# Windowed attention and a routed MLP: stores on GpSimd's queue, an early identity, full-width transposes, and two more engines in program order

## The chip, the cores and the metric

The kernel runs on one core of a Trainium2 chip. TensorE multiplies matrices, VectorE and ScalarE do element-wise work, GpSimd does slower general work and issues some DMAs, and SyncE only issues DMAs. Each engine works through its own list of instructions in order and waits on semaphores for the others. The metric is the time of one launch in microseconds (us), as the median of several runs. The profile is one such execution, and its times count from the start of its span.

## The reference

Four batches of eight heads, 768 positions, 64 numbers a head. Each query sees itself, the 127 positions before it, and four "sink" positions at the start. A routed MLP then works on 128 rows of each batch.

```python
scores = scale * np.matmul(q, k.transpose(0, 1, 3, 2))
keep = is_sink | in_window
a = softmax(np.where(keep, scores, -1e9))
x = np.matmul(a, v)                          # heads side by side: [B, S, 512]
scores = np.einsum('bsd,d->bs', x, w_gate)
for b in range(B):
    top_idx = np.argpartition(-scores[b], capacity)[:capacity]
    xe = x[b, top_idx]
    ye = np.maximum(xe @ w1, 0.0) @ w2
    out[b, top_idx] = x[b, top_idx] + sigmoid(scores[b, top_idx])[:, None] * ye
```

The rows that aren't chosen go out as x.

## The kernel before, in words

**Units.** The attention is cut in 24 units (b, j): batch b, block j of 128 queries. In unit u the loop gives out, in this order: at j = 0 the loads of the next batch (`load_qk`, `load_v`, and for batch 0 three weight loads); the scores of the *next* unit, whose exponentials ScalarE writes into `pt` (L274); the sink part of the output (`pv_sinks`, L291); the casts of the next batch's q and k for the head pairs that `prep` names; the output product `pv` for two groups of four heads (L301), each followed by VectorE's reciprocal `rz` (L307) and product `x` (L310); the sink scores at j = 0; the transposes of the next batch; two casts of MLP weights in units (1,0) to (1,3) (`cast_w`, L212 and L215); `compare` for the unit before; one step of the MLP of the batch before (`moe_steps`); and `finish_block`.

**Casts and transposes.** q and k come in as 32-bit numbers (`kf`, `qf`) and are cast to bf16 (`kb`, `qb`), two heads to a tile: by ScalarE and VectorE for batch 0 (L107, L108), by GpSimd with a select that selects everything for the others (L111). TensorE then turns each 128x64 piece (L227), one head into the upper and one into the lower 64 partitions of a PSUM tile; VectorE copies the turned k out (`KT`, L232, and a small piece `ksk`, L236), ScalarE the turned q (`QT`, L234).

**Sinks.** `load_v` loads v in six pieces (L120). After the second it also loads the sink rows `vsr` (L126, two small loads), and VectorE multiplies them with a selection mask into `vsk` (L127), which `pv_sinks` reads from j = 2 on:

```python
            if c == 1:
                raw = vsr[b % 2]
...
                nc.vector.tensor_tensor(
                    out=st.vsk[:, :, 0:D], in0=raw[:, :].unsqueeze(1).to_broadcast((128, 4, D)),
```

**Finish and choice.** `finish_block` stores x (L315), for the last batch also makes a bf16 copy on GpSimd (L319), and reduces x with the gate weights to a score per row (`junk`, `scol`, L322). `compare` spreads the scores over the partitions (`bc` by TensorE, `sbc` by ScalarE, L330) and counts on VectorE which rows rank higher (`cm`, L333). The steps of `moe_steps` run in units j = 1 to 5 of the next batch: the ranks and a selection matrix `E` (L345 to L358); the row numbers `idx` and the gather of the chosen rows from the output in memory (`xe`, L374, by GpSimd); their transposes `xeT` (L380); the two products (L390, L396); and a gated add to memory (L400). `moe_last` does it for the last batch.

**Buffers.** x has four buffers, the accumulators `xg` three, other PSUM tiles five, raw q and k three each, `kb` and `qb` three each, v and `vsr` two.

**What sets the order.** In the loop, TensorE's instructions keep the order in which the program gives them. All other engines, and SyncE's DMA queue, are ordered by a planner: it models the run, and at each step gives an engine the earliest instruction of the program that it then holds to be ready. The instructions ahead of the loop are all ordered by it. All loads and stores are issued by SyncE; the gathers and scatters by GpSimd.

```python
    with tc.manual_schedule(engines={ENG.PE}):
        start_state(st0)
        keep_warm(14)
```

`keep_warm` (L76) gives TensorE empty products, to keep its clock up.

Of the kernel before, what the change touches and what calls it, by code (L numbers as in the profile page):

```python
# [10 lines left out]
BF16 = mybir.dt.bfloat16  # L11
# [3 lines left out]
ALU = mybir.AluOpType  # L15
ENG = mybir.EngineType
# [4 lines left out]
D = 64  # L21
HP = H // 2
NB = S // 128
# [8 lines left out]
def kernel(  # L32
# [13 lines left out]
    nc = tc.nc  # L46

    cp = ctx.enter_context(tc.tile_pool(name="cp", bufs=1))
# [3 lines left out]
    qbp = ctx.enter_context(tc.tile_pool(name="qbp", bufs=3))  # L52
# [20 lines left out]
    def keep_warm(n):  # L73
        w = ps.tile([128, 512], FP32, name="w", tag="ps")
        for _ in range(n):
            nc.tensor.matmul(out=w[:, :], lhsT=warm[:, 0:128], rhs=warm[:, :], start=True, stop=True)  # L76
# [4 lines left out]
    def load_qk(b, parts):  # L81
        st = BatchState()
        st.b = b
        st.kq = {}
        st.qf, st.kf = [], []
        n = 4 // parts
        for g in range(2):
            for lst, nm in ((st.kf, "kf"), (st.qf, "qf")):
                lst.append(qkp.tile([128, 4, NB, D], FP32, name=nm, tag=nm))
            for i in range(parts):  # L90
                for src, lst in ((k, st.kf), (q, st.qf)):
                    h0 = 4 * g + n * i
                    nc.sync.dma_start(
                        out=lst[g][:, n * i:n * i + n, :, :].rearrange("p h c d -> p h (c d)"),
                        in_=src[b, h0:h0 + n, :, :].rearrange("h (p c) d -> p h (c d)", c=NB))
        return st

    def casts(st, hp):
        kb = qbp.tile([128, 2, NB, D], BF16, name="kb", tag="kb")
        qb = qbp.tile([128, 2, NB, D], BF16, name="qb", tag="qb")  # L100
        h0 = 2 * (hp % 2)
        ks = st.kf[hp // 2][:, h0:h0 + 2, :, :].rearrange("p h c d -> p (h c d)")
        qs = st.qf[hp // 2][:, h0:h0 + 2, :, :].rearrange("p h c d -> p (h c d)")
        ko = kb[:, :, :, :].rearrange("p h c d -> p (h c d)")
        qo = qb[:, :, :, :].rearrange("p h c d -> p (h c d)")
        if st.b == 0:
            nc.scalar.copy(out=ko, in_=ks)  # L107
            nc.vector.tensor_copy(out=qo, in_=qs)  # L108
        else:
            for o, i in ((ko, ks), (qo, qs)):  # L110
                nc.gpsimd.affine_select(out=o, in_=i, compare_op=ALU.is_ge, fill=0.0, base=0,  # L111
                                        pattern=[[0, 2 * NB * D]], channel_multiplier=0)
        st.kq[hp] = (kb, qb)

    def load_v(st):
# [15 lines left out]
    st0 = load_qk(0, 2)  # L131


    ident_f = cp.tile([128, 128], FP32, name="ident_f", tag="ident_f")
    make_identity(nc, ident_f)
    ident_b = cp.tile([128, 128], BF16, name="ident_b", tag="ident_b")
    nc.vector.tensor_copy(ident_b[:], ident_f[:])  # L137
    for i in range(2):
        nc.vector.memset(vsr[i][:, :], 0.0)
        nc.vector.memset(ksk[i][:, :, :], 0.0)  # L140
# [4 lines left out]
    for R in range(2):  # L145
        o = sel[64 * R:64 * R + 64, :]
        nc.gpsimd.affine_select(out=o, in_=o, compare_op=ALU.is_ge, fill=0.0, base=0,
                                pattern=[[-4, 4]], channel_multiplier=1)
        nc.gpsimd.affine_select(out=o, in_=o, compare_op=ALU.is_ge, fill=0.0, base=3,
                                pattern=[[4, 4]], channel_multiplier=-1)  # L150
# [8 lines left out]
    for e in range(2):  # L159
        rows = trif[64 * e:64 * e + 64]  # L160
        nc.gpsimd.affine_select(out=rows[:, 2, :], in_=rows[:, 2, :], compare_op=ALU.is_ge,
                                fill=MASK_NEG, base=0, pattern=[[1, 64]], channel_multiplier=-1)
        nc.gpsimd.affine_select(out=rows[:, 0, :], in_=rows[:, 0, :], compare_op=ALU.is_ge,
                                fill=MASK_NEG, base=-1, pattern=[[-1, 64]], channel_multiplier=1)
    msk = cp.tile([128, 2, 3, 64], BF16, name="msk", tag="msk")
    nc.vector.tensor_copy(out=msk[:, :, :, :], in_=trif[:, :, :].unsqueeze(1).to_broadcast((128, 2, 3, 64)))
    for e in range(2):
# [12 lines left out]
                            fill=-1e-30, base=0, pattern=[[-1, 128]], channel_multiplier=1)  # L180
# [28 lines left out]
    def cast_w(i):  # L209
        src = wf[i // 2][:, 1024 * (i % 2):1024 * (i % 2) + 1024]  # L210
        if i < 4:
            nc.scalar.copy(out=w1_sb[:, i, :], in_=src)  # L212
        else:
            fs = slice(2 * (i - 4), 2 * (i - 4) + 2)
            nc.scalar.copy(out=w2_sb[:, fs, :].rearrange("p a n -> p (a n)"), in_=src)  # L215


    def transposes(st, hp):
        if not hasattr(st, "QT"):
            st.QT = tp.tile([128, HP, S], BF16, name="QT", tag="QT")  # L220
            st.KT = tp.tile([128, HP, S], BF16, name="KT", tag="KT")
            st.ksk = ksk[st.b % 2]
        for t, (src, dst) in enumerate(((st.kq[hp][0], st.KT), (st.kq[hp][1], st.QT))):
            trp = ps.tile([128, 8, 128], BF16, name="trp", tag="ps")
            for c in range(NB):
                for e in range(2):
                    nc.tensor.transpose(out=trp[64 * e:64 * e + 64, c, :],  # L227
                                        in_=src[:, e, c, :], identity=ident_b[:])
            o = dst[:, hp, :].rearrange("d (p c) -> d p c", c=NB)
            i = trp[:, 0:NB, :].rearrange("d c p -> d p c")  # L230
            if t == 0:
                nc.vector.tensor_copy(out=o, in_=i)  # L232
            else:
                nc.scalar.copy(out=o, in_=i)  # L234
        for e in range(2):
            nc.vector.tensor_copy(  # L236
                out=st.ksk[64 * e:64 * e + 64, hp, 8 * (hp % 2) + 4 * e:8 * (hp % 2) + 4 * e + 4],
                in_=st.KT[64 * e:64 * e + 64, hp, 0:NSINK])
# [73 lines left out]
            in0=xg[:, :, 0:D], in1=rz[:, :, :].to_broadcast((128, 4, D)), op=ALU.mult)  # L312

    def finish_block(st, j):
        nc.sync.dma_start(out=out[st.b, j * 128:(j + 1) * 128, :], in_=st.x[:, :])  # L315
        if st.b == B - 1:
            if j == 0:
                st.xb = ws.tile([128, NB, DM], BF16, name="xb", tag="wf")
            nc.gpsimd.affine_select(out=st.xb[:, j, :], in_=st.x[:, :], compare_op=ALU.is_ge, fill=0.0,  # L319
                                    base=0, pattern=[[0, DM]], channel_multiplier=0)  # L320
        junk = sp.tile([128, DM], FP32, name="junk", tag="junk")
        nc.vector.tensor_tensor_reduce(  # L322
            out=junk[:, :], in0=st.x[:, :], in1=wgb[:, :], scale=1.0, scalar=0.0,
            op0=ALU.mult, op1=ALU.add, accum_out=st.scol[:, j:j + 1])
# [158 lines left out]
    def start_state(st):  # L483
        st.pt = {}
        st.cm = {}
        st.scol = sp.tile([128, NB], FP32, name="scol", tag="scol")
        st.row = sp.tile([128, NB], FP32, name="row", tag="row")
        st.sbc = sp.tile([128, S], FP32, name="sbc", tag="sbc")

    states = {0: st0}  # L490
    units = [(b, j) for b in range(B) for j in range(NB)]
    with tc.manual_schedule(engines={ENG.PE}):
        start_state(st0)
        keep_warm(14)
        for g in range(2):
            for hp in (2 * g, 2 * g + 1):
                casts(st0, hp)
                transposes(st0, hp)
                keep_warm(4)
            scores(st0, 0, g)  # L500
        gen = None
        prep = {True: {2: (0,), 3: (1, 2), 4: (3,)}, False: {1: (0,), 2: (1,), 3: (2,), 4: (3,)}}
        for u, (b, j) in enumerate(units):
            st = states[b]
            if j == 0 and b + 1 < B:
                states[b + 1] = load_qk(b + 1, 2 if b == 0 else 1)
                load_v(states[b + 1])
                if b == 0:
                    for i in range(3):
                        load_w(i)  # L510
            nxt = units[u + 1] if u + 1 < len(units) else None
            if nxt:
                if nxt[1] == 0:
                    start_state(states[nxt[0]])
                for g in range(2):
                    scores(states[nxt[0]], nxt[1], g)
            pv_sinks(st, j)
            hps = prep[b == 0].get(j, ()) if b + 1 < B else ()
            for hp in hps:
                casts(states[b + 1], hp)  # L520
            for g in range(2):
                pv(st, j, g)
            if j == 0:
                sink_scores(st)
            for hp in hps:
                transposes(states[b + 1], hp)
            if b == 1 and j < 4:
                cast_w(2 * j)
                cast_w(2 * j + 1)
                if j == 0:  # L530
                    load_w(3)
            if u:
                pb, pj = units[u - 1]
                compare(states[pb], pj)
            if gen is not None:
                if next(gen, "end") == "end":
                    gen = None
            finish_block(st, j)
            if j == 0 and b > 0:
                gen = moe_steps(states[b - 1])  # L540
        moe_last(states[B - 1])
# [35 lines left out]
```

The softmax here doesn't subtract the row's maximum and nothing guards it: scores larger than these inputs give would overflow.

## Time and profile before

The time was 164.15 us, the median of 3 runs (162.9 to 165.42). The profiled execution has a span of 162.8 us.

| engine | busy us | share of the span |
|---|---|---|
| TensorE, matmuls | 132.8 | 82% |
| TensorE, weight loads | 100.8 | 62% |
| VectorE | 100.4 | 62% |
| ScalarE | 86.9 | 53% |
| GpSimd | 39.7 | 24% |

31.82 MB were moved, 29.66 MB of them by SyncE's queue. In a line of the timeline the columns are start, duration, engine, line, operation and tiles, and in brackets the idle time before it and who ended it; in the chain they are start, duration, and what the end of the run hung on in that stretch. "SPq" is SyncE's queue, and its durations are those of the issue, not of the transfer. "PE" is TensorE, "DVE" VectorE, "ACT" ScalarE and "POOL" GpSimd. "Issue" is time in which an engine waited for nothing that the profile shows.

### The profile page before, as it was taken

The numbers are of one execution on the slowest core, as the hardware profiler recorded it, in microseconds if no ns is written. First come the engines' busy times: TensorE is split into PE (matmuls) and PEld (weight loads), VectorE is DVE, ScalarE is ACT, GpSimd is POOL, SyncE is SP. The second block draws the span as 40 slices with busy tenths as digits, with TensorE's granted clock in tenths as the row PEclk, the third lists the DMA queues.
The fourth block names the chain that finished last, engine by engine and source line by source line (L and its number), as shares of the span: only waits on it lengthen the run. The fifth ranks groups of instructions, "written<-read, shape, count | busy, mean of one in ns | idle before, by whom it ended". The sixth has DMA issues, their size and how long they took to land.

```text
span 162.8 us, 6953 instructions
## 1 busy us (share of the span) xinstructions
PE 132.8 (82%) x3053; PEld 100.8 (62%) x3053; DVE 100.4 (62%) x306; ACT 86.9 (53%) x172; POOL 39.7 (24%) x57
## 2 busy tenths in 40 slices
PE   6659995958726997790599999999999996999960
PEld 2235583846614885680398668787877885875730
DVE  3177645659713799974128787977767876756310
ACT  3156695446269675351908495656749664412120
POOL 6000005720000536330044233020006142224202
PEclk9969999999975899999569999999999999999996
DMA  5999999989999869899987999041113514113221
GB/s 173 266 366 192 199 260 385 282 193 273 349 340 392 289 195 315 184 224 281 392 319 218 251 185 266 25 96 68 68 64 35 164 68 104 66 39 51 44 68 64
DMA packets 39951, 31.82 MB, mean 195 GB/s; under 512 B 26096, under 2 KB 34672, under 8 KB 39920
## 3 DMA queue, kind: packets, MB, share of 16 engines
q1 hardware_dynamic: 38896, 29.66, 62.3%
q0 software_dynamic: 1024, 1.70, 6.3%
q8 instruction: 24, 0.39, 1.0%
q14 instruction: 7, 0.06, 0.1%
HBM read 24.41 MB, written 7.34 MB: 195 GB/s over the span
## 4 chain that ended last, share of the span: by engine, by line
PE 51%; DMA 21%; DVE 13%; issue 8%; ACT 2%; SPq 1%; POOLq 1%; POOL 0%
PE xg L301 21%; DMA xe<-out_dram,idx 8%; DMA out_dram<-x 7%; PE w L76 6%; PE sc L257 5%; DMA qf<-in_q_dram 4%; PE xg L291 4%; PE trp L227 4%; DVE x L310 3%; PE hps L390 3%; DVE KT L232 3%; PE ye L396 3%; PE sc L268 2%; DMA xr<-out_dram,idx 2%; DVE cm L333 2%
## 5 line engine op out<-in xcount | busy, mean ns | idle before, releaser
L274 ACT ACTIVATE pt<-sc 128x512 f32<-128x512 f32 (+1 forms) x96 | 46.9, 578 | 10.1 <-PE sc L268 10.0
L301 PEld LDWEIGHTS xg<-vbuf,pt 128*64 128x64 f32 x1408 | 45.9, 145 | 9.5 <-issue 7.9
L301 PE MATMUL xg<-vbuf,pt 128*64 128x65 f32 x1408 | 49.5, 231 | 1.0 <-issue 0.7
L307 DVE RECIPROCAL rz<-xg 128x4 f32<-128x4 f32 x48 | 8.7, 180 | 29.2 <-PE xg L301 28.8
L234 ACT COPY QT<-trp 128x768 bf16<-128x768 bf16 x16 | 12.7, 800 | 24.0 <-PE trp L227 24.0
L111 POOL TENSOR_SCALAR_AFFINE_SELECT kb<-kf 128x768 bf16<-128x768 f32 x12 | 9.8, 825 | 63.1 <-DMA kf<-in_k_dram 38.1
L310 DVE TENSOR_TENSOR x<-xg,rz 128x256 f32<-128x256 f32 x48 | 20.3, 424 | 6.2 <-DMA out_dram<-x 4.6
L257 PE MATMUL sc<-QT,KT 64*64 64x192 bf16 (+3 forms) x384 | 19.0, 248 | 5.2 <-DVE KT L232 2.9
L333 DVE SCALAR_TENSOR_TENSOR cm<-sbc,scol,tie 128x128 bf16<-128x128 f32 (+5 forms) x24 | 18.3, 763 | 6.2 <-ACT sbc L330 6.0
L322 DVE CUSTOM_DVE_ANT_0 junk<-x,wgb 128x512 f32<-128x512 f32 x24 | 19.5, 814 | 0.8 <-DMA wgb<-in_moe_w_gate_dram 0.6
L268 PE MATMUL sc<-msk,ident_b 64*64 64x256 bf16 (+1 forms) x352 | 17.0, 246 | 3.4 <-issue 3.4
L76 PE MATMUL w<-warm 128*128 128x512 bf16 x53 | 16.0, 451 | 1.3 <-DVE warm L71 1.3
L232 DVE COPY KT<-trp 128x768 bf16<-128x768 bf16 x16 | 15.1, 950 | 1.9 <-PE trp L227 1.7
L257 PEld LDWEIGHTS <-KT 64*64 64x64 bf16 x384 | 9.4, 107 | 11.1 <-issue 9.0
L291 PE MATMUL xg<-vsk,psk 64*64 64x260 f32 x128 | 12.2, 412 | 3.4 <-DVE x L310 3.4
L268 PEld LDWEIGHTS <-ident_b 64*64 64x64 bf16 x352 | 10.6, 108 | 3.9 <-issue 3.9
L330 ACT COPY sbc<-bc 128x128 f32<-128x128 f32 x24 | 6.5, 272 | 10.7 <-PE bc L329 10.7
L111 POOL TENSOR_SCALAR_AFFINE_SELECT qb<-qf 128x768 bf16<-128x768 f32 x12 | 10.7, 905 | 6.2 <-DMA qf<-in_q_dram 6.2
L227 PE MATMUL trp<-ident_b,kb 128*64 128x128 bf16 x192 | 8.7, 225 | 3.4 <-DVE ident_b L137 3.1
L76 PEld LDWEIGHTS <-warm 128*128 128x128 bf16 x53 | 5.3, 111 | 8.0 <-issue 3.9
L227 PEld LDWEIGHTS <-kb 128*64 128x64 bf16 x192 | 6.7, 113 | 5.3 <-issue 5.1
L319 POOL TENSOR_SCALAR_AFFINE_SELECT xb<-x 128x512 bf16<-128x512 f32 x6 | 5.8, 962 | 15.1 <-DVE x L310 15.0
(97 smaller groups left out, 144.0 us busy)
## 6 DMA issues: line engine op xcount, KB each, us to landing
vbuf<-in_v_dram SPq DMA_DIRECT2D x24, 256.0 KB, 4.9
out_dram<-x SPq DMA_DIRECT2D x24, 256.0 KB, 6.3
wf<-in_moe_w_dram SPq DMA_DIRECT2D x4, 1024.0 KB, 8.9
kf<-in_k_dram SPq DMA_DIRECT2D x8, 384.0 KB, 8.9
qf<-in_q_dram SPq DMA_DIRECT2D x8, 384.0 KB, 8.0
kf<-in_k_dram SPq DMA_DIRECT2D x4, 768.0 KB, 11.8
qf<-in_q_dram SPq DMA_DIRECT2D x4, 768.0 KB, 6.0
wgb<-in_moe_w_gate_dram SPq DMA_DIRECT2D x1, 256.0 KB
```

Source lines behind the costliest of these rows:

```text
L76: nc.tensor.matmul(out=w[:, :], lhsT=warm[:, 0:128], rhs=warm[:, :], start=True, stop=True)
L111: nc.gpsimd.affine_select(out=o, in_=i, compare_op=ALU.is_ge, fill=0.0, base=0, pattern=[[0, 2 * NB * D]], channel_multiplier=0)
L227: nc.tensor.transpose(out=trp[64 * e:64 * e + 64, c, :], in_=src[:, e, c, :], identity=ident_b[:])
L232: nc.vector.tensor_copy(out=o, in_=i)
L257: nc.tensor.matmul(out=sc[e][es[kh], hh, q0:q1], lhsT=st.KT[es[e], hp, k0:k0 + 64], rhs=st.QT[es[e], hp, kc * 128 + q0:kc * 128 + q1], sta ...
L268: nc.tensor.matmul(out=sc[e][es[kh], :, 64 * s0:64 * s1].rearrange("p h (s n) -> p h s n", n=64), lhsT=ident_b[es[e], es[e]], rhs=m[es[e], ...
L274: nc.scalar.activation(out=po[:, e, :, 0:nq], in_=sc[e][:, :, 0:nq], func=ACT.Exp, scale=0.125)
L291: nc.tensor.matmul(out=st.xg[g][es[m], :, :], lhsT=st.psk[es[g], q0:q0 + 64], rhs=st.vsk[es[g], :, :], start=True, stop=False, skip_group_ ...
L301: nc.tensor.matmul(out=xg[es[m], hh, :], lhsT=st.pt[kc][:, h, off + 64 * m:off + 64 * m + 64], rhs=st.v[:, kc, h, :], start=(j < 2 and hh ...
L310: nc.vector.tensor_tensor(out=st.x[:, 256 * g:256 * g + 256].rearrange("p (h d) -> p h d", h=4), in0=xg[:, :, 0:D], in1=rz[:, :, :].to_bro ...
L322: nc.vector.tensor_tensor_reduce(out=junk[:, :], in0=st.x[:, :], in1=wgb[:, :], scale=1.0, scalar=0.0, op0=ALU.mult, op1=ALU.add, accum_ou ...
L333: nc.vector.scalar_tensor_tensor(out=cm[:, :], in0=st.sbc[:, 0:n], scalar=st.scol[:, j:j + 1], in1=tie[:, S - n:S], op0=ALU.subtract, op1= ...
```

## The change

Four things change. The store of x is issued by GpSimd in place of SyncE. The bf16 identity, which every transpose needs, is made at once by GpSimd, ahead of the 32-bit one, and no longer copied from it by VectorE. The bf16 tiles of q and k are laid out block by block with the two heads side by side, so that one full 128x128 transpose takes the place of two 128x64 ones; the casts write that layout, and GpSimd's take two instructions, one a head. And in the loop VectorE and ScalarE, too, keep the order of the program. This last is for a set order of the work in place of the planner's, the first for stores that don't stand in line with the loads.

```diff
     def casts(st, hp):
-        kb = qbp.tile([128, 2, NB, D], BF16, name="kb", tag="kb")
-        qb = qbp.tile([128, 2, NB, D], BF16, name="qb", tag="qb")
+        kb = qbp.tile([128, NB, 2, D], BF16, name="kb", tag="kb")
+        qb = qbp.tile([128, NB, 2, D], BF16, name="qb", tag="qb")
...
-        ko = kb[:, :, :, :].rearrange("p h c d -> p (h c d)")
+        ko = kb[:, :, :, :].rearrange("p c h d -> p h c d")
...
             for o, i in ((ko, ks), (qo, qs)):
-                nc.gpsimd.affine_select(out=o, in_=i, compare_op=ALU.is_ge, fill=0.0, base=0,
-                                        pattern=[[0, 2 * NB * D]], channel_multiplier=0)
+                for e in range(2):
+                    nc.gpsimd.affine_select(out=o[:, e, :, :], in_=i[:, e, :, :], compare_op=ALU.is_ge, fill=0.0,
+                                            base=0, pattern=[[0, NB], [0, D]], channel_multiplier=0)
...
+    ident_b = cp.tile([128, 128], BF16, name="ident_b", tag="ident_b")
+    make_identity(nc, ident_b)
     ident_f = cp.tile([128, 128], FP32, name="ident_f", tag="ident_f")
     make_identity(nc, ident_f)
-    ident_b = cp.tile([128, 128], BF16, name="ident_b", tag="ident_b")
-    nc.vector.tensor_copy(ident_b[:], ident_f[:])
...
             for c in range(NB):
-                for e in range(2):
-                    nc.tensor.transpose(out=trp[64 * e:64 * e + 64, c, :],
-                                        in_=src[:, e, c, :], identity=ident_b[:])
+                nc.tensor.transpose(out=trp[:, c, :], in_=src[:, c, :, :].rearrange("p h d -> p (h d)"),
+                                    identity=ident_b[:])
...
     def finish_block(st, j):
-        nc.sync.dma_start(out=out[st.b, j * 128:(j + 1) * 128, :], in_=st.x[:, :])
+        nc.gpsimd.dma_start(out=out[st.b, j * 128:(j + 1) * 128, :], in_=st.x[:, :])
...
-    with tc.manual_schedule(engines={ENG.PE}):
+    with tc.manual_schedule(engines={ENG.PE, ENG.DVE, ENG.Activation}):
```

## The prediction

> **What bounds the kernel now.** I read the chain that ended last first, in order of time. TensorE leads it with 51% and DMA holds 21%, but that DMA share lies in three or four places, and two of them are long:
>
> ```profile
> 37.35 0.41 DVE vsk L127
> 37.76 0.33 DVE x L310
> 38.09 0.88 DVE KT L232
> 38.97 0.03 issue
> 38.99 10.72 DMA out_dram<-x
> 49.72 0.02 issue
> 49.74 0.44 DVE x L310
> ...
> 69.62 9.50 DMA xe<-out_dram,idx
> 79.11 0.05 issue
> 79.16 0.61 PE xeT L380 x4
> ```
>
> The fifth block of batch 0 waits for a free x buffer (four of them), that is for a store; unit (1,3) waits for the gathered rows. The timeline of SyncE's queue says why the store is late:
>
> ```profile
> 18.67 0.43 SPq L93 DMA_DIRECT2D kf<-in_k_dram  x1
> ...
> 23.07 0.37 SPq L93 DMA_DIRECT2D qf<-in_q_dram  x1
> 24.46 4.19 SPq L120 DMA_DIRECT2D vbuf<-in_v_dram  x2
> 28.70 3.24 SPq L126 DMA_DIRECT2D vsr<-in_v_dram  x2
> 31.98 3.75 SPq L120 DMA_DIRECT2D vbuf<-in_v_dram  x4
> 35.78 3.12 SPq L207 DMA_DIRECT2D wf<-in_moe_w_dram  x3
> 38.99 2.19 SPq L315 DMA_DIRECT2D out_dram<-x  x4
> ```
>
> The first store's data is ready at 22.5 us; it is issued at 38.99, behind every load of batch 1 and 3 MB of weights. The stretches show DMA at 0.98 to 1.09 of its time from 10 to 50 us and 0.99 from 58 to 80: the first 80 us are bound by loading, and what a transfer queues behind sets when it lands. From 100 us TensorE is busy 9.7 to 10 of each 10 us up to 130.
>
> The second thing to see is where VectorE does line 127, the small product that makes vsk of the next batch. It starts at 18.71, 37.35, 66.89 and 94.10 us and never waits. The planner put the one for batch 1 after the first half of unit (0,3), although the program has it ahead of the outputs of (0,0), which ran at 21.37.
>
> **What the Trainium skill says.** "DMA: Bandwidth & Descriptors", section "Issuing engines are not separate DMA queues", says that DMAs of all queues run on the same 16 engines and that another issuer saves only the issue time. The trace agrees in this: the gather, alone on GpSimd's queue, took 9.5 us at 69.62 and 3.5 to 3.6 later, when DMA was light. Its section "SWDGE vs HWDGE vs iDMA" says each DMA engine goes round-robin between its queues; that 9.5 doesn't look like much of a fair share. "TensorE: Matmul & The Clock Gate", Part 3, says small tiles in different parts of the array overlap; the trace shows it in the transposes below.
>
> **The change, part by part.** *Transposes.* Two column halves become one full one: 384 become 192. The chain has both kinds, warm:
>
> ```profile
> 84.94 0.67 PE trp L227 x24
> 85.61 0.25 PE bc L329
> 85.87 1.79 PE hps L390 x32
> ```
>
> 24 half transposes take 0.67 us, 28 ns each, since the halves run beside each other. 32 full 128x128 bf16 products take 1.79, 56 ns each. Twelve full ones: 12 x 56 = 0.67 us. Gain 0; the bounds are 0 and half, 16 x 0.33 = 5.4 us. I take 0.
>
> *Casts.* GpSimd's 128x768 takes 0.82 us and its 128x128 f32 0.28; the line through them gives 0.18 + 0.84 ns an element, so 384 elements take 0.50 and a pair 1.0. That is 24 x 0.18 = 4.3 us more on an engine busy 39.7 of 162.8, and hidden: kb of batch 2 was cast at 53.88, its transposes came after 61. For batch 0 the strided copies keep runs of 64 elements; I put them at 0 to 0.2 us and take 0, since ScalarE and VectorE wait over 6 us there for k and q.
>
> *Early identity.* TensorE waited 3.1 us for ident_b until 9.98, while kb (cast 3.83 to 4.66) and qb (5.97 to 6.53) were there. With it, the first transposes start at 6.6. Later pairs wait for q and k to land (qb of the second pair at 9.10), so about 2.8 us remain at the first scores. Whether it survives depends on the next part.
>
> *Stores by GpSimd.* It takes the store out of SyncE's line: the wait that ends at 49.74 loses its cause. Chain piece 10.7 us; VectorE was idle for 4.6 of it and TensorE for 3.4, beside 1.7 of instruction issue. Each issue costs GpSimd some 1.0 to 1.6 us, as its indirect ones (the skill's page has 1 us to the first byte): 24 x 1.2 = 29 us on an engine with 123 idle. It bites once: the last gather by moe_steps follows x of (3,2) at 132.1, and a store goes in ahead of it; the queue then holds 256 KB before the gather's rows. I take 1 us, bounds 0 and 2.5.
>
> *VectorE in program order.* It adds a wait. load_v of the next batch stands ahead of the unit's outputs, so its line 127 now blocks VectorE until vsr has landed, and behind it queue rz and x of units (0,0) on; TensorE waits for those, having three xg buffers: it gets through pv(0,0) and half of pv(0,1).
> Batch 1: vsr's two loads were issued from 28.70 to 31.94, the second at about 30.3; v's loads in that stretch landed 4.0 to 5.6 us after issue. So 34.3 to 35.9; I take 34.5. The SyncE order until then holds no store, so I expect it unchanged. Outputs of (0,0) come at 35 instead of 21.4: 13.6 us lost, and the 2.8 of the early identity with them. Then units of some 4.7 us (rows at 103.6, 108.2, 112.8), the first ones shorter as TensorE is ahead: (0,1) 37.5, (0,2) 41, (0,3) 46, (0,4) 50.5, (0,5) 55.5. Before, (0,5) ended at 55.3: the new wait takes just about what the freed stores give back. Sum so far 0.
> Batch 2: vsr comes in SyncE's order after 3 MB of weights, 3.15 MB of q and k and 0.5 MB of v. At 39 us the weights are still to come. With 1.3 MB of stores beside them that is 8.0 MB; at 345 to 380 GB/s (352 was seen from 39 to 50), v slower (some 210), about 22 us: it lands near 61. VectorE gets there at 55.5 + cm 1.0 + junk 0.7 = 57.2. Wait 3.8; the first output of (1,0) comes at 61.6, against 58.18: +3.4.
> Batch 3: its vsr is asked for by 75 and landed by 90, before VectorE comes to it near 95: 0.
>
> *ScalarE in program order.* The weight casts, 8 of 1.06 us, ran from 47.15 to 53.9 inside the store wait, six of them. Now two stand in each unit (1,0) to (1,3), ahead of that unit's sbc, which cm waits for. After the transposes ScalarE needs 0.80 + 2 x 1.06 + 0.27 = 3.2 us; VectorE comes to cm after x, KT, ksk, some 1.9. So 1.3 us a unit, in stretches where VectorE is the fuller engine (11.73 of 12 us busy from 58 to 70). Two units to (1,2): 1.3 to 2.6, I take 1.4.
>
> *The gather of batch 0.* Before, issued at 69.62, landed at 79.11. Now issued 69.6 + 3.4 + 1.4 + 0.6 (idx stands after KT, ksk, cm) = 75. Loads of batch 3 are then in line, so between 3.6 and 9.5 us; I take 7: 82. TensorE itself is there at 79. Against 79.11: +2.9.
>
> *From there to the end* as before: TensorE-bound, the same order of work. In moe_last two rid products come ahead of the last picks: +0.2.
>
> Sum: 2.9 + 1 + 0.2 = +4.1; 164.15 + 4.1 = 168.3, called 168.
>
> **Rivals.** *Both later waits are hidden* (faster, 0.27): vsr of batch 2 lands before 57 because the queues share better, and the gather takes 3.6 to 5. Then the rows arrive at 75 to 76, when TensorE comes: 79.1 becomes 75.5, its clock doesn't drop (0.77 granted from 80 to 90, worth 1 to 2 us), +1.2 at the end: 159 to 161. For it: light gathers took 3.5. Against: DMA at 0.99.
> *Only the gather is quick* (no change, 0.27): +3.4 and +1.4 stay, TensorE is at xeT near 79, no wait there: 164 to 166.
> *GpSimd's queue gets in the way* (slower still, 0.12): a cast waiting for its k or q stands ahead of a store or of the gather. GpSimd waited 38.1 us for k before, 19.9 at once. Should kb of batch 3 stand ahead of the gather, 3 to 6 us come on top: 171 to 175. Against: a cast has the later place in the program.
> *The forecast* (0.34): 166 to 170.
>
> **How the numbers follow.** The forecast and the last rival give slower, less a tenth where the sum falls under 167.4: 0.45. The first rival gives faster: 0.27. The rest is 0.28. The range reaches from the middle of the first rival, 159, to the first half of the last, 173.
>
> **What would show it.** Right: line 127 of batch 1 on VectorE at 33 to 36 us with an idle of over 12 us before it put down to a DMA of vsr, and x of (0,0) after it; no wait of x on a store; a second idle of 2 to 6 us before line 127 near 61; pairs of weight casts in four units; 12 transposes still taking 0.6 to 0.7; xeT waiting for xe near 80. Wrong: line 127 finding its data landed (vsr issued ahead of q and k, or landing past the queue), then the gain of the stores and the identity stands and the time falls to 155 or so; or a full transpose at 28 ns; or GpSimd issuing stores late.

## The result, and the profile after

The changed kernel takes 172.56 us (median of 4 runs, 171.18 to 173.72), against 163.53 (4 runs, 161.64 to 165.42) for the kernel before alongside. The ratio is 1.063, 95% interval 1.046 to 1.080: slower, by more than twice the forecast 2.3%. Every ratio here and below compares only the faster executions of each kernel, those within 1.5% of its quickest, so it can differ from the quotient of the two medians that stand beside it. The profiled span went from 162.8 to 172.0 us.

The direction and the first mechanism are what was forecast. In the chain that ended last, in order of time, of the kernel after, the store wait is gone, and the sink rows and the first gather stand in it:

```profile
28.65 3.39 SPq L127
32.08 2.21 DMA vsr<-in_v_dram
34.38 0.42 DVE vsk L128
...
34.93 0.42 DVE x L310
...
77.63 0.76 DVE cm L333 x2
...
78.94 5.78 DMA xe<-out_dram,idx
```

Line numbers are one higher than before from the casts on: the vsk product, line 127 before, is line 128 now. It ends the wait for `vsr`, and the outputs of (0,0) follow at once. The gather that started at 69.62 now starts at 78.94. The product runs once a batch. On VectorE's timeline (start, duration, and in brackets the idle time before and its cause) those of batches 0, 1 and 2 wait:

```profile
16.37 0.42 DVE L128 TENSOR_TENSOR vsk<-vsr,sel 128x256 f32<-128x256 f32 x1 [4.32 <-DMA vsr<-in_v_dram]
...
34.38 0.42 DVE L128 TENSOR_TENSOR vsk<-vsr,sel 128x256 f32<-128x256 f32 x1 [14.50 <-DMA vsr<-in_v_dram]
...
62.22 0.42 DVE L128 TENSOR_TENSOR vsk<-vsr,sel 128x256 f32<-128x256 f32 x1 [0.24 <-DMA vsr<-in_v_dram]
```

Together they are 19.1 us of idle VectorE, where before this product never waited. SyncE's queue issues the rows for batch 1 at 28.65 us, as the chain shows, and those for batch 2 only here (start and length of the issue):

```profile
55.60 3.56 SPq L127 DMA_DIRECT2D vsr<-in_v_dram  x2
```

The page's line for the store, among the groups (total us and mean ns between the bars), and its line in the DMA issues (KB, median us to landing), say what the store costs where it is now:

```profile
L315 POOL DMA_DIRECT2D out_dram<-x x24 | 13.6, 567 | 45.2 <-DVE x L310 43.7
...
out_dram<-x POOLq DMA_DIRECT2D x24, 256.0 KB, 3.6
```

An issue takes 0.57 us of GpSimd, and the store lands after 3.6 us; on SyncE's queue it took 6.3 in the kernel before. (In order_only below, with the stores still on SyncE's queue, it takes 3.0, so the change of queue is not all of that difference.)

Where the 9.2 us of span come from is read from the same work in both traces, as the delay of after against before:

| event | before | after | delay |
|---|---|---|---|
| first `rz` of (0,0) | 21.4 | 34.7 | 13.4 |
| first `rz` of (1,0) | 58.2 | 62.6 | 4.4 |
| first `rz` of (1,3) | 71.7 | 79.7 | 8.0 |
| `xeT` of batch 0 | 79.16 | 84.76 | 5.6 |
| first `rz` of (3,0) | 123.2 | 129.1 | 5.9 |
| first `rz` of (3,2) | 130.5 | 137.4 | 6.9 |
| products `hps` of batch 2 | 140.23 | 148.83 | 8.6 |

So 4.4 us are there when batch 1 starts; 3.6 more build up until (1,3), of which the shorter landing of the gather (5.8 us against 9.5) gives some back; batch 2 only carries the delay; and batch 3 adds 2.7.

### The profile page after: what moved, and what is told of

Same layout as the page of the kernel before. It is cut to its first block, busy times and chain, and to the rows that moved or that the text cites. A ratio compares the mean times of both kernels' runs of the same rounds, so it can differ in the third digit from the quotient of the medians.

```text
span 172.0 us, 6586 instructions
## 1 busy us (share of the span) xinstructions
PE 135.0 (78%) x2861; PEld 103.6 (60%) x2861; DVE 100.2 (58%) x305; ACT 85.8 (50%) x172; POOL 59.2 (34%) x107
## 4 chain that ended last, share of the span: by engine, by line
PE 41%; DMA 20%; ACT 12%; DVE 11%; SPq 9%; issue 5%; POOLq 1%; DVEq 0%; ACTq 0%
PE xg L301 18%; DMA qf<-in_q_dram 9%; DMA xe<-out_dram,idx 8%; ACT pt L274 5%; PE xg L291 4%; SPq L127 3%; PE hps L390 3%; SPq L121 3%; PE sc L257 3%; PE ye L396 3%; PE trp L227 3%; ACT QT L234 3%; PE w L76 3%; DVE cm L333 2%; DMA xr<-out_dram,idx 2%
## 5 line engine op out<-in xcount | busy, mean ns | idle before, releaser
L301 PE MATMUL xg<-vbuf,pt 128*64 128x65 f32 x1408 | 52.4, 237 | 10.7 <-DVE rz L307 8.6
L301 PEld LDWEIGHTS xg<-vbuf,pt 128*64 128x64 f32 x1408 | 48.5, 150 | 19.4 <-issue 18.2
L315 POOL DMA_DIRECT2D out_dram<-x x24 | 13.6, 567 | 45.2 <-DVE x L310 43.7
L112 POOL TENSOR_SCALAR_AFFINE_SELECT kb<-kf 128x384 bf16<-128x384 f32 x24 | 12.6, 549 | 47.2 <-DMA kf<-in_k_dram 31.3
L257 PE MATMUL sc<-QT,KT 64*64 64x192 bf16 (+3 forms) x384 | 19.9, 257 | 5.5 <-ACT sbc L330 2.4
L112 POOL TENSOR_SCALAR_AFFINE_SELECT qb<-qf 128x384 bf16<-128x384 f32 x24 | 14.5, 630 | 1.7 <-DMA qf<-in_q_dram 1.0
L128 DVE TENSOR_TENSOR vsk<-vsr,sel 128x256 f32<-128x256 f32 x4 | 1.7, 424 | 19.1 <-DMA vsr<-in_v_dram 19.1
L227 PE MATMUL trp<-ident_b,kb 128*128 128x128 bf16 x96 | 8.1, 220 | 4.1 <-ACT kb L107 4.1
L291 PE MATMUL xg<-vsk,psk 64*64 64x260 f32 x128 | 11.2, 411 | 0.0
L227 PE MATMUL trp<-ident_b,qb 128*128 128x128 bf16 x96 | 8.3, 225 | 2.2 <-DVE qb L108 2.2
```

Source lines behind the costliest of these rows:

```text
L112: nc.gpsimd.affine_select(out=o[:, e, :, :], in_=i[:, e, :, :], compare_op=ALU.is_ge, fill=0.0, base=0, pattern=[[0, NB], [0, D]], channel ...
L227: nc.tensor.transpose(out=trp[:, c, :], in_=src[:, c, :, :].rearrange("p h d -> p (h d)"), identity=ident_b[:])
L257: nc.tensor.matmul(out=sc[e][es[kh], hh, q0:q1], lhsT=st.KT[es[e], hp, k0:k0 + 64], rhs=st.QT[es[e], hp, kc * 128 + q0:kc * 128 + q1], sta ...
L291: nc.tensor.matmul(out=st.xg[g][es[m], :, :], lhsT=st.psk[es[g], q0:q0 + 64], rhs=st.vsk[es[g], :, :], start=True, stop=False, skip_group_ ...
L301: nc.tensor.matmul(out=xg[es[m], hh, :], lhsT=st.pt[kc][:, h, off + 64 * m:off + 64 * m + 64], rhs=st.v[:, kc, h, :], start=(j < 2 and hh ...
```

## The experiments

Every ratio is against the kernel before on the same chip. Where none is given, no interval came out of the runs, and medians and ranges stand in its place. Edits are to the kernel after unless another is named.

### The parts, one at a time

**stores_only**: the kernel before with only the issuer of the store changed.

```diff
-        nc.sync.dma_start(out=out[st.b, j * 128:(j + 1) * 128, :], in_=st.x[:, :])
+        nc.gpsimd.dma_start(out=out[st.b, j * 128:(j + 1) * 128, :], in_=st.x[:, :])
```

> The kernel before with only the store of x issued by GpSimd. Theory: the wait of x of (0,4) on a store (10.7 us in the chain, 4.6 of idle VectorE) goes, and so does part of it later: 155 to 161. Rival 2 (stores on GpSimd cost more than they give): 163 to 168.

Measured: 162.81 against 164.77 us, ratio 0.982 (0.977 to 0.987). The stores alone are a gain of 1 to 2% (1.2% by the medians), far less than the 10.7 us in the old chain. In its trace no x waits for a store.

**transposes_only**: the identity, the layout of `kb` and `qb`, and the full transposes, with the store on SyncE and the planner's order.

```diff
-        nc.gpsimd.dma_start(out=out[st.b, j * 128:(j + 1) * 128, :], in_=st.x[:, :])
+        nc.sync.dma_start(out=out[st.b, j * 128:(j + 1) * 128, :], in_=st.x[:, :])
...
-    with tc.manual_schedule(engines={ENG.PE, ENG.DVE, ENG.Activation}):
+    with tc.manual_schedule(engines={ENG.PE}):
```

> The kernel before with only the early identity, the new layout of kb and qb with its casts, and full transposes. Theory: the first scores come 2 to 3 us earlier, and twelve full transposes take 0.79 us in the changed kernel's chain against 0.67 for 24 halves, 1.9 us in all; the store wait at 39 to 50 us ends when it ended: no change, 162 to 166. Rival 2: the transposes cost 3 us or more, 166 to 169.

Measured: 164.36 against 164.77 us, ratio 0.997 (0.987 to 1.007). No measurable difference.

**order_only**: the kernel before with only this line changed.

```diff
-    with tc.manual_schedule(engines={ENG.PE}):
+    with tc.manual_schedule(engines={ENG.PE, ENG.DVE, ENG.Activation}):
```

> The kernel before with only VectorE and ScalarE put in program order; stores by SyncE, late identity and half transposes stay. Theory: VectorE waits for vsr of batch 1 until 34 to 36 us as in the changed kernel, and the store wait at 39 to 50 us vanishes by itself since the x of (0,4) comes only near 51: 170 to 175. Rival 1: the same, 170 to 175. Rival 2: half of the loss or less, 164 to 168.

Measured: 180.15 us (177.53 to 181.41) against 164.77. By the medians the order alone costs 9.3%; the kernel after, which has the other changes too, is 6.3% slower. Stores, identity and transposes together are worth 3 points inside the ordered kernel, though these two were not measured side by side. Its gather of batch 0 was issued only at 88.00 and took 4.8 us. No x waits for a store here either, with the stores still on SyncE's queue: the order alone takes that wait away.

**no_order** and **order_act**: the kernel after with the planner's order back on both engines, and on VectorE alone.

```diff
-    with tc.manual_schedule(engines={ENG.PE, ENG.DVE, ENG.Activation}):
+    with tc.manual_schedule(engines={ENG.PE})                       # no_order
+    with tc.manual_schedule(engines={ENG.PE, ENG.Activation})       # order_act
```

> The changed kernel with only TensorE in program order, so stores, identity and transposes are changed and VectorE and ScalarE are the planner's. If the parts add up (0.982 for the stores alone, 0.997 for the transposes alone): 158 to 163, and the whole loss is that of the order. If the parts hinder each other: 165 or more.

> The changed kernel with TensorE and ScalarE in program order and VectorE left to the planner. Theory A (VectorE's order carries the loss, by vsk and by its fixed order later): within 2 us of the kernel with neither, 158 to 164. Theory B (ScalarE's order carries it, by the weight casts ahead of sbc): 168 to 173.

Measured: no_order 164.32 against 163.68 us, 0.990 (0.979 to 1.002); order_act 162.6 against 163.68, 0.982 (0.973 to 0.992). The whole loss goes when VectorE is given back to the planner; ScalarE in program order does no harm by itself. On VectorE's timeline of order_act the products for batches 1 and 2 start at 37.31 and 67.36 us, later than in the kernel after, and wait for nothing.

### The place of the vsk product

**vsk_late**: VectorE stays in program order, but the product of batches 1 to 3 is given out at the end of unit j = 1 of its own batch, just ahead of its first reader.

```diff
+                if b == 0:
+                    sink_values(st)
...
+    def sink_values(st):
         nc.vector.tensor_tensor(
...
             finish_block(st, j)
+            if j == 1 and b > 0:
+                sink_values(st)
```

> The changed kernel, but with the product that makes vsk of batches 1 to 3 given out at the end of unit j = 1 of its own batch, just ahead of its first reader, in place of inside load_v. Theory (VectorE blocked at vsr of batch 1 is the main cost): outputs of unit (0,0) start near 20 us and the time falls by 10 us or more, to 155 to 162. Rival 1 (ScalarE's program order, with the weight casts ahead of sbc, and the slower units are the main cost): the run is bound by loading anyway and stays at 168 to 173. Rival 2 (the stores or the full transposes cost): 165 to 168.

Measured: 178.07 (176.91 to 179.66) against 164.77 us, 1.090 (1.073 to 1.107): worse still. Its first `rz` of (1,0) came at 48.0 us, 14.5 ahead of the kernel after, so the block was indeed gone; but a new wait took its place. The waits (us in total, times, longest us) and the chain of this kernel:

```profile
PE xg L295 <- DVE vsk L132: 10.1, 3, 3.9
```

```profile
63.45 0.68 DVE junk L326
...
64.14 0.35 DVE vsk L132
...
64.53 1.15 PE xg L295 x8
65.67 3.35 PE xg L305 x64
```

The sink products of j = 2 are early in TensorE's order, while the product stood at the end of unit j = 1 on VectorE, behind `E` and `junk`. TensorE waited three times, and then ran the 64 products in 3.35 us that otherwise take 2.02. So this run says nothing on whether the block mattered; the next one does.

**vsk_mid**: the same, right after x of unit j = 1, ahead of the unit's other work on VectorE. **vsk_mid_act_free**: the same with ScalarE back with the planner.

```diff
             for g in range(2):
                 pv(st, j, g)
+            if j == 1 and b > 0:
+                sink_values(st)
```

> The changed kernel with the vsk product of batches 1 to 3 right after the x products of unit j = 1 of its own batch, ahead of KT and cm, so that it neither blocks unit (0,0) nor keeps TensorE's sink products waiting, as it did for 10 us at the end of that unit. Theory A: the 4.4 us that the changed kernel had lost by unit (1,0) come back, and up to 2 more: 164 to 169. Theory C (the run is bound by loading until unit (2,0), so being early gains nothing): 171 to 174.

> The same, with ScalarE left to the planner, so only TensorE and VectorE keep the program's order. Theory A: 2 us or less under the one before. Theory B: 4 us or more under it, since the six weight casts can run before unit (1,0) and sbc isn't held up: 158 to 163.

Measured: vsk_mid 166.27 against 163.68 us, 1.017 (1.009 to 1.025); vsk_mid_act_free 163.15, 0.995 (0.989 to 1.001). Moving one product of 0.42 us, in three batches, takes 1.063 to 1.017, each against runs of the kernel before taken beside it: the largest piece. With it moved, ScalarE's order is worth another 2 points, and these two were measured side by side.

In vsk_mid (1,0) comes at 49.8 us, 12.7 ahead of the kernel after, yet (3,0) only 6.5 ahead, at 122.6. From (1,0) to (1,5) it takes 39.0 us, where the kernel after takes 33.1: much of an early start is given back in batch 1. In vsk_late GpSimd's first cast for batch 2 had its k only at 52 us; that loading limits batch 1 is the reading, not a separate test.

### ScalarE's casts and the place of the step

Edits to vsk_mid. **casts_late** puts the two weight casts of a unit behind `compare` and the MLP step; **steps_first** puts the MLP step ahead of `compare`; **both_moved** does both.

```diff
-            if b == 1 and j < 4:                 # casts_late: moved down
-                cast_w(2 * j)
...
             if u:
                 pb, pj = units[u - 1]
                 compare(states[pb], pj)
             if gen is not None:                  # steps_first: moved above compare
                 if next(gen, "end") == "end":
                     gen = None
+            if b == 1 and j < 4:
+                cast_w(2 * j)
...
```

> The changed kernel with the vsk product moved as in vsk_mid (1.017 of the time before), and the two weight casts of units (1,0) to (1,3) given out after compare and the step of moe_steps, so that sbc no longer stands behind them on ScalarE. If the casts ahead of sbc, for which cm and so VectorE wait, are what ScalarE's order costs there: 0.99 to 1.005, as with ScalarE left to the planner (0.995). If ScalarE's order costs by something else: 1.01 to 1.02.

> vsk_mid with the step of moe_steps given out ahead of compare, so that E, idx and with it the gather come ahead of cm on VectorE. If the fixed place of idx behind cm makes the gathers late, xe comes 0.5 to 1 us earlier in each of three batches, with the clock drop after the wait in batch 3: 1.00 to 1.012. If not: 1.012 to 1.022.

> Both moves on top of vsk_mid: the order by hand with its three misplaced pieces put elsewhere. If the two effects add: 0.975 to 0.995, as fast as stores alone or as ScalarE in order with VectorE free (0.982 both). Rival (a fixed order on VectorE costs by itself, wherever these stand): 0.995 to 1.01.

Measured: casts_late 164.52 against 164.24 us, 1.011 (1.003 to 1.019); steps_first 169.45, 1.034 (1.025 to 1.044); both_moved 168.72 (164.41 to 170.07) against 164.24, far from what was expected of it.

The casts do cost something in the trace: `xeT` of batch 0 comes at 75.17 in casts_late and at 78.02 in vsk_mid. In time it is 1.011 against 1.017, with intervals that overlap. That doesn't account for all of the 2 points that freeing ScalarE gives.

steps_first was meant to bring the gather forward, and failed. The waits of it, and then of vsk_mid:

```profile
DVE cm L337 <- ACT sbc L334: 21.4, 12, 4.0
```

```profile
DVE cm L337 <- ACT sbc L334: 11.6, 7, 3.0
```

VectorE waits 9.8 us more for `sbc`. TensorE's `bc`, which `sbc` copies, now stands behind the step's matrix products in TensorE's order too. That this is the cause is argued from the order, not tested apart.

### The stretch of batch 3

From (3,0) to `hps` of batch 2 the kernel after lost 2.7 us, 1.0 of them in (3,0) to (3,2), which takes 8.2 us in place of 7.3. Two theories for that part: `junk` standing behind `cm`'s wait, or the small products on `row` and `rid` that stand in unit (b+1, 1).

**junk_first**: casts_late with `finish_block` of j = 0 moved ahead of the casts and `compare`. **junk_first_all**: for every unit. **junk_first_act_free**: vsk_mid_act_free with `finish_block` of j = 0 moved.

```diff
+            if j == 0:                # junk_first_all: for every j
+                finish_block(st, j)
...
-            finish_block(st, j)
+            if j:
+                finish_block(st, j)
```

> casts_late (1.011 of the time before) with the store and the score product junk of units j = 0 given out ahead of compare, so that VectorE has it to do while cm waits for sbc, which on ScalarE stands behind four exponentials and psk. If the fixed place of cm ahead of junk makes VectorE the bound at the start of each batch (120 to 127 us of the chain in vsk_mid_act_free): 0.5 to 1 us from each of three batches and the clock drop in batch 3, 0.99 to 1.003. If an order by hand costs otherwise: 1.005 to 1.015.

> The same in every unit, so idx, too, stands behind junk. If junk ahead of idx delays the gathers by its 0.7 us: 1 to 2 us over the one before. If what counts is only that VectorE has work while cm waits: the same as the one before.

> vsk_mid with that junk moved at j = 0, and ScalarE left to the planner (with junk in its old place 0.995). If the effects add: 0.975 to 0.988, at least as fast as ScalarE in order with VectorE free (0.982). If not: 0.99 to 1.0.

Measured, against 164.88 us (160.83 to 166.26): 164.18 (161.95 to 165.86), 165.94 (165.04 to 168.59) and 164.11 (160.54 to 167.33). No effect can be told, and in junk_first (3,0) to (3,2) still took 8.6 us. The first theory falls. What fills the stretch shows on VectorE's timeline of junk_first:

```profile
126.50 1.01 DVE L353 TENSOR_TENSOR row<-row,behind 128x5 f32<-128x5 f32 x1
...
127.81 0.96 DVE L356 TENSOR_TENSOR E<-iota_f,row 128x768 bf16<-128x768 f32 x1
128.68 0.17 DVE L361 TENSOR_SCALAR rid<-scol 128x6 bf16<-128x6 f32 x1
128.89 0.17 DVE L362 SCALAR_TENSOR_TENSOR rid<-scol,rid 128x6 bf16<-128x6 f32 x1
128.97 0.68 DVE L326 CUSTOM_DVE_ANT_0 junk<-x,wgb 128x512 f32<-128x512 f32 x1
```

`cm` ended at 126.58, so 2.4 us lie between it and `junk`. In the kernel before the planner had done the first `row` product and both on `rid` ahead of this stretch, at 121.78, 121.90 and 122.11 us; between `cm` and `junk` only one small product stood:

```profile
128.37 0.16 DVE L350 TENSOR_TENSOR row<-cs,row 128x5 f32<-128x5 f32 x1
128.44 1.02 DVE L322 CUSTOM_DVE_ANT_0 junk<-x,wgb 128x512 f32<-128x512 f32 x1
```

**rows_early**: the kernel after with these three given out at the end of unit (b, 5), where their data is complete. **rows_early_moved**: junk_first with the same. **rows_early_act_free**: rows_early_moved with ScalarE back with the planner, and the weight casts where the kernel after has them.

```diff
+            if j == NB - 1 and b + 1 < B:
+                rows_ready(st)       # row + behind, and the two products on rid
```

> The changed kernel with three small VectorE products of the first MLP step (behind added to row, the two rid products) given out at the end of unit (b,5), when their inputs are there, in place of unit (b+1,1). If they are what fills VectorE in that unit and so makes the gather late (0.97 + 0.17 + 0.17 us ahead of the next outputs, the later wait for xe and the clock drop after it in batch 3): (3,0) to (3,2) takes 7.3 to 7.6 us in place of 8.3, the time falls by 1.5 to 4 us, 1.04 to 1.055. If not: 1.055 to 1.07.

> The same on top of junk_first (vsk product, weight casts and junk of j = 0 moved; its (3,0) to (3,2) took 8.6 us). If it is these products: 7.3 to 7.8 us there, and 0.975 to 0.99. If not: 0.99 to 1.003.

> The same with ScalarE left to the planner. If the parts add: 0.97 to 0.985, the fastest of all. If not: 0.985 to 1.0.

Measured, against 165.69 us (162.46 to 169.33): rows_early 171.02, 1.042 (1.037 to 1.047); rows_early_moved 161.38, 0.986 (0.981 to 0.992); rows_early_act_free 163.05, 0.987 (0.981 to 0.994). In rows_early (3,0) to (3,2) takes 7.2 us, and `hps` of batch 2 starts at 146.98 instead of 148.83. That is 1.85 us or 1.1% in the trace, and 2 points in the ratios, whose intervals touch. But 1.3 of the 1.85 us are there at (3,0) already (127.8 for 129.1): the products were moved in every batch, and most of the gain comes in batch 2. In rows_early_moved it starts at 139.32, ahead of the 140.23 of the kernel before.

With these pieces moved (vsk, casts, rows, and `junk` of j = 0) the kernel in program order beats the kernel before, and freeing ScalarE then gains nothing. order_act, stores_only and rows_early_moved beat both kernels by about as much, 0.982 to 0.986, each on another chip.

## Why the prediction was right or wrong, step by step

The sum of the forecast was 4.1 us, 2.9 of them until `xeT` of batch 0 and 1.2 from there to the end. Measured in the span are 9.2: 5.6 and 3.6. The direction and the first mechanism were right; the terms that were too small are named below.

**The block at the vsk product: right.** Forecast 34.5 us after 13.6 lost; measured 34.38 after 14.5 idle. Units (0,1) to (0,3) came at 36.6, 40.9 and 45.5, for 37.5, 41 and 46. vsk_mid shows that the place of this product is what costs most: 4.6 of the 6.3 points.

**The forecast that it is paid back by (0,5): wrong, a term put at 0.** (0,4) and (0,5) came at 51.5 and 56.7, for 50.5 and 55.5, and the second half of (0,5) at 59.27 after 1.94 us idle. In the kernel before that half came at 54.63, so the kernel was 4.6 us behind here, where I had 0. I took 4.7 us a unit; 4.7 to 6.0 was measured in the stretch where the transposes of batch 1 stand in the units, and TensorE lost 0.42 and 1.40 us in it to instruction issue.

**The second wait: right result by luck.** `vsr` of batch 2 landed near 62, forecast 61, but VectorE itself came only then and idled 0.24 us, not 3.8. (1,0) is 4.4 us late, for 3.4, but by the slow units of batch 0, not by this wait. Had the loads been quicker, little would have been gained at this product.

**ScalarE's order in batch 1: the term was mis-sized.** I put 1.4 us on the way to (1,2). `cm` waited for `sbc` 0.92, 0.72 and 1.14 us in units (1,0) to (1,2), 2.8 in sum, and the gather was issued 9.3 us late, where I had 5.4. The third of these waits, on ScalarE's timeline:

```profile
75.44 1.99 ACT L216 CAST w_sb<-wf 128x1024 bf16<-128x1024 f32 x2
77.33 0.27 ACT L330 COPY sbc<-bc 128x128 f32<-128x128 f32 x1
```

The copy of `bc` stands behind two casts, exactly as worked out; I priced two units where three were on the way to the gather. But casts_late shows that the casts are only part of it. The 0.6 us for `idx` behind `KT`, `ksk` and `cm` was too small as well: in the kernel before `idx` followed `KT` at once, at 69.18, and now `ksk` (0.97 us) and `cm` (0.75) stand between, beside the wait.

**The gather: right in kind.** It took 5.8 us, inside 3.6 to 9.5, near my 7; issued 3.9 us later than I had it, it puts `xeT` 5.6 us late instead of 2.9. This term, with the one before, is where half of the missing time is.

**"From there to the end as before", with 1 us for the store ahead of the last gather and 0.2 for rid: this step failed.** In batch 3 alone 2.7 us came on top. They fall into three parts. The first is VectorE's: I saw the two rid products only in `moe_last`, and priced them at 0.2; but in `moe_steps` they and the first `row` product also come to stand in unit (b+1, 1) on VectorE, ahead of `junk` and x. On VectorE's timeline of the kernel after:

```profile
134.44 0.16 DVE L349 TENSOR_TENSOR row<-row,behind 128x5 f32<-128x5 f32 x1
...
134.91 1.65 DVE L352 TENSOR_TENSOR E<-iota_f,row 128x768 bf16<-128x768 f32 x1
136.48 0.16 DVE L357 TENSOR_SCALAR rid<-scol 128x6 bf16<-128x6 f32 x1
...
136.76 0.69 DVE L322 CUSTOM_DVE_ANT_0 junk<-x,wgb 128x512 f32<-128x512 f32 x1
```

Up to `idx` (132.35 before, 138.87 after) this stretch adds 0.6 us to the delay. The second part is the gather's: from `idx` to `xeT` it takes 4.85 us in place of 4.30, with GpSimd's store of x now ahead of it. That is the term that I had at 1 us. The third and largest part is TensorE's speed after the wait for the gathered rows. Its timeline in the kernel before, and after:

```profile
136.65 0.40 PE L380 MATMUL xeT<-ident_b,xe 128*128 128x128 bf16 x4 [1.28 <-DMA xe<-out_dram,idx]
...
137.89 2.09 PE L301 MATMUL xg<-vbuf,pt 128*64 128x65 f32 x64
```

```profile
143.72 0.40 PE L380 MATMUL xeT<-ident_b,xe 128*128 128x128 bf16 x4 [2.05 <-DMA xe<-out_dram,idx]
...
144.95 3.62 PE L301 MATMUL xg<-vbuf,pt 128*64 128x65 f32 x64
```

The wait is 0.8 us longer, and the 64 products after it take 1.5 longer. The granted clock from 140 to 150 us is 0.83, where the kernel before had 1.00. I had put nothing for this. But the longer wait doesn't settle it. In order_act TensorE waits as long at the same place and keeps its clock:

```profile
132.71 0.40 PE L380 MATMUL xeT<-ident_b,xe 128*128 128x128 bf16 x4 [2.11 <-DMA xe<-out_dram,idx]
...
133.94 2.09 PE L301 MATMUL xg<-vbuf,pt 128*64 128x65 f32 x64
```

So what makes the clock drop in one kernel and not in the other stays open, and these 1.5 us can't be put down to the order of work alone.

**Transposes, casts, identity: right.** Twelve full transposes, on TensorE's timeline of the kernel after, from their start to that of `bc`:

```profile
41.67 0.51 PE L227 MATMUL trp<-ident_b,kb 128*128 128x128 bf16 x6
...
42.35 0.28 PE L329 MATMUL bc<-ident_f,scol 128*128 128x128 f32 x1
```

0.68 us, forecast 0.67, and transposes_only is at 0.997. The early identity is eaten by a wait that I had not named, the vsk product of batch 0 (4.32 us until 16.37), and again by the one at 34.38.

**Stores: right in direction.** No x waits for a store any more, though order_only shows that in this order none would have waited anyway. An issue costs 0.57 us where I had 1.2. In the trace no engine waits for a cast of GpSimd; the gather of batch 0 is issued 0.5 us after `idx` is done, for 0.3 before. That rival with its 3 to 6 us is out, though its time, 171 to 175, is the one that came.

**The chances.** The forecast's 0.34 and the last rival's 0.12, less a tenth, are 0.41 to 0.43 and not the 0.45 that I put for slower.

What stays open: why TensorE's clock drops after the last gather in some of these kernels; what in ScalarE's order, beside the casts, cost the rest of the 2 points, and why that is gone once the rows are moved; and how much of an early start loading takes back in batch 1.

## What to carry to other kernels

To write an engine's order by hand is to promise that each instruction's data is there when its turn comes. Go through the program for consumers of a DMA that are written where the load is, not where the value is needed: the place of one small product was worth 4.6 points here. Then look for small instructions that a planner had slipped into idle time, and for the reader: an instruction moved late (vsk_late) can hold up a second engine that is also in fixed order. And when a delay lets TensorE wait, read the granted clock behind the wait: a drop can cost more than the wait (1.5 us against 0.8 here), but the length of the wait alone doesn't foretell it.

## What the runs showed of the hardware

VectorE's products with two inputs in SBUF, the on-chip working memory, get longer beside GpSimd's copies and casts. Over the 19 traces `junk`, which is such a product, never took more than 0.74 us in the 305 cases in which none of these overlapped it, and more than 0.8 us in 122 of the 151 in which one did; the x product, which has one input in PSUM, never took more than 0.43. In the kernel after, `E` took 1.65 us at 134.91, where it takes 0.95 alone; GpSimd's copy of x to bf16 ran for 0.64 us from 135.10. In junk_first the 128x5 product of 0.16 us took 1.01 and ended at 127.51; GpSimd's copy ran from 126.85 to 127.48. In rows_early the copy was the longer one, 0.97 us, beside an `E` of 0.96. The Trainium skill's "SBUF — State Buffer", section "SBUF: two separate sides", says that VectorE and GpSimd share one pair of ports as an exclusive lock, taken by VectorE's products with two inputs in SBUF too, and that the loser waits. The sums agree (0.95 + 0.64 = 1.59 for 1.65). The page also says that whoever starts first keeps the pair; here `E` started first by the trace and was still the longer one, though by 0.19 us only, and GpSimd's times in a trace are rough.

The Trainium skill's "TensorE: Matmul & The Clock Gate", Part 1, puts the drop of the clock at an idle window of about 3.4 us. Around the gather in batch 3 no wait was that long. Yet in nine of the 19 traces the mean granted clock in the 7 us around it was 0.76, after waits of 1.12 to 2.79 us (the two shortest with another gap of 0.4 to 0.6 us just ahead), and in ten it stayed at 1.00, after waits of 1.20 to 2.20. The small products around the wait may count as near idle, which no run tells apart.
